# Where GpSimd puts its first sum: in its own room, or in the one that VectorE has just read

## The chip, the cores and the metric
The kernel runs on one core of one Trainium2 chip. The metric is the device time in microseconds. Three runs of the kernel before gave 2311.27, 2308.0 and 2311.83 us, median 2311.27 us. A further execution was taken with a profile, and its trace is what the views below show.

## The reference
An attention with 32 inducing points per batch is followed by a feed-forward layer with a rational activation:

```
s = scale * (I @ x^T);  h = softmax(s) @ x          # 4 batches, 12480 rows, 128 columns
y = softmax(scale * (x @ h^T)) @ h                   # 49920 rows in all
u = y @ w_in                                         # 128 -> 2048
g = (a0 + a1 u + a2 u^2 + a3 u^3) / (1 + |b0| |u| + |b1| u^2 + 1e-6)
out = g @ w_out                                      # 2048 -> 128
```

All of it is in float32, and the second part has most of the work.

## The kernel before
The 49920 rows are cut into 104 blocks of 480. A block's 2048 hidden columns are cut into eight units of 256, so there are 832 units, each a [128, 2, 480] tile. The loop `fast_ticks` takes one unit per tick `t`.

For unit `t`, TensorE writes u (folded with the attention, so that its input is the softmax weights) into one of three PSUM buffers named `hp`, one tick ahead. The absolute value goes into a slot of `row`: on VectorE where `t` is even (the `mask`, an integer AND), on ScalarE where it is odd. One tick later VectorE makes the unit's polynomial part, (row + k1) * hp, and puts it into a rung of `line`; that frees the `hp` buffer. `row` and `line` have twenty slots each and are used in a ring, so slot and rung of unit `i` are written again for unit `i+20`.

ScalarE then works on the slots of four units at a time: a logarithm and later a sigmoid, in place, three logarithms and three sigmoids for every twelve units, with two loads of the function table (`wide`).

In tick `i+17` (`BEHIND` is 17), for each four units `i` to `i+3`, `finals` makes line = (line + k3) * row. I call it the final of these units. VectorE makes that of the first two units in one instruction of 128x1920 elements, which reads two operands from SBUF. GpSimd makes that of the other two, unit by unit, with two instructions each: a sum (`tensor_scalar`, 128x960) and a product (`tensor_tensor`, 128x960). For the last four groups VectorE makes all of them. Two ticks after unit `i+2`'s own delay, in tick `i+21`, TensorE multiplies its rung with `w_out` into the buffer `po` (`second`); unit `i+3` follows in tick `i+22`.

The engines take their instructions in the order in which the program issues them; semaphores that the framework places from the overlap of the regions read and written are all that orders one engine against another. What is left over in a tick is given, in `side`, to work on the next batch: attention scores, exponentials, the quotient `a`/`asm` (on GpSimd: a small sum and a product), the stack `st` of the next weights (on GpSimd: a cast and a difference) and the transfers. The program fixes the order of all that when it is built, with costs written in the code.

The change is in `finals`. Before, the two GpSimd instructions of a unit both write the unit's rung `u.g`: the sum in place, and then the product of it with the slot `u.u`.

Of the kernel before, what the change touches and what calls it, by code (L numbers as in the profile page):

```python
# [17 lines left out]
ALU = mybir.AluOpType  # L18
# [187 lines left out]
class Kernel:  # L206
# [932 lines left out]
    def finals(self, units, i):  # L1139

        V, G, p = self.nc.vector, self.nc.gpsimd, self.params
        part = units[i:i + 4]
        own = 4 if i + BEHIND > len(units) else 2
        for k in range(0, min(own, len(part)), 2):
            a, b = part[k], part[min(k + 1, own - 1)]
            g, w = self.line[:, a.rung:b.rung + 1], self.row[:, a.slot:b.slot + 1]
            V.scalar_tensor_tensor(out=g, in0=g, scalar=p.z_k3, in1=w, op0=ALU.add, op1=ALU.mult)
        for u in part[own:]:
            G.tensor_scalar(out=u.g, in0=u.g, scalar1=1.0, scalar2=p.z_k3, op0=ALU.mult, op1=ALU.add)
            G.tensor_tensor(out=u.g, in0=u.g, in1=u.u, op=ALU.mult)  # L1150

    def general_ticks(self, units):
        V, A, G, p = self.nc.vector, self.nc.scalar, self.nc.gpsimd, self.params
# [172 lines left out]
```

## Time and profile before

| what | value |
|---|---|
| median of three runs | 2311.27 us (2308.0 to 2311.83) |
| the profiled execution's own time | 2307.58 us |
| its span, first to last instruction | 2305.7 us |
| granted TensorE clock, mean | 0.986 of full speed |
| VectorE busy | 2219.0 us, 96% |
| TensorE busy | 2130.3 us, 92% |
| ScalarE busy | 2061.2 us, 89% |
| GpSimd busy | 1786.6 us, 77% |

In the rows PE is TensorE, DVE is VectorE, ACT is ScalarE, POOL is GpSimd. A row of a timeline has the start in us from the start of the span, the duration in us, engine, line, operation, out<-in with the tiles' names, and in brackets the idle time of the engine before it and what ended that. A row of groups has the count, the busy time in us and the mean duration in ns. Nearly all instructions are issued through one helper, so all have its line, L190, and are told apart by tiles.

### The profile page before, as it was taken

Reading aid. Unit: us, or ns where it says so; the run is one execution under the profiler, and the core shown is the slowest. Engines: PE = TensorE matmul, PEld = TensorE weight load, DVE = VectorE, ACT = ScalarE, POOL = GpSimd, SP = SyncE. Lnnn points to the kernel's source line nnn. Section 1 sums busy time; section 2 is a strip of 40 time slices with the busy share of each in tenths; the row PEclk is TensorE's granted clock in tenths of the full one; section 3 lists DMA queues with packets and bytes.
Section 4 is the critical chain, followed back from the end, with each engine's and each line's share of the span. In section 5 each row is a group of like instructions: output and inputs, shape, how many; then the busy total and the mean of one; then the engine's idle time right before and its main releaser. Section 6 shows DMA issues by size and latency. Waiting matters only on the chain.

```text
span 2305.7 us, 22902 instructions
## 1 busy us (share of the span) xinstructions
PE 2130.3 (92%) x7728; PEld 967.6 (42%) x7728; DVE 2219.0 (96%) x2094; ACT 2061.2 (89%) x1085; POOL 1786.6 (77%) x1040
## 2 busy tenths in 40 slices
PE   5599999988999999998999999999999999999998
PEld 2244444434444444444444444444444444444444
DVE  7899999999999999999999999999999999999996
ACT  2589998988998999898998999999999999989996
POOL 1378687868887688788888768889887888878883
PEclk8799999999999999999999999999999999999999
DMA  8422031101223123100122203110110010000000
GB/s 313 129 69 68 24 89 48 35 29 41 69 73 90 35 55 84 36 22 30 35 88 88 73 22 86 48 40 18 55 48 17 22 52 19 25 18 22 18 18 19
DMA packets 105153, 125.03 MB, mean 54 GB/s; under 512 B 13378, under 2 KB 101314, under 8 KB 104514
## 3 DMA queue, kind: packets, MB, share of 16 engines
q1 hardware_dynamic: 105026, 123.48, 17.1%
q8 instruction: 63, 1.03, 0.2%
q14 instruction: 64, 0.52, 0.1%
HBM read 84.04 MB, written 26.61 MB: 48 GB/s over the span
## 4 chain that ended last, share of the span: by engine, by line
DVE 44%; PE 32%; issue 16%; ACT 4%; POOL 2%; DMA 1%; SPq 1%; DVEq 0%; POOLq 0%; ACTq 0%
DVE line L190 26%; PE po L190 21%; DVE row L190 11%; PE hp L190 8%; ACT row L190 3%; DVE oT L190 2%; POOL line L190 2%; PE ph L190 1%; DVE a L190 1%; PE pd L190 1%; PE pc L190 1%; DVE amx L190 1%; DVE hl L190 1%; DVE asm L190 1%; SPq L190 0%
## 5 line engine op out<-in xcount | busy, mean ns | idle before, releaser
L190 PE MATMUL po<-line,w_out 128*128 128x480 f32 x3328 | 1553.0, 572 | 3.9
L190 POOL TENSOR_TENSOR line<-line,row 128x960 f32<-128x960 f32 x408 | 1031.8, 2529 | 282.3 <-ACT row L190 229.3
L190 DVE SCALAR_TENSOR_TENSOR line<-row,all,hp 128x960 f32<-128x960 f32 x832 | 996.1, 1203 | 12.3 <-PE hp L190 11.0
L190 PEld LDWEIGHTS po<-line,w_out 128*128 128x128 f32 x3328 | 616.3, 190 | 404.5 <-issue 244.3
L190 ACT ACTIVATE row<-row,all 128x3840 f32<-128x3840 f32 x208 | 725.7, 3490 | 0.0
L190 ACT ACTIVATE row<-row 128x3840 f32<-128x3840 f32 x208 | 706.6, 3397 | 1.3 <-DVE line L190 1.3
L190 POOL TENSOR_SCALAR line<-line,all 128x960 f32<-128x960 f32 x408 | 668.5, 1639 | 3.6
L190 DVE SCALAR_TENSOR_TENSOR line<-line,all,row 128x1920 f32<-128x1920 f32 x212 | 608.6, 2873 | 19.9 <-ACT row L190 19.6
L190 PE MATMUL hp<-at,st 128*128 128x480 f16 x1664 | 477.0, 368 | 119.8 <-DVE line L190 112.2
L190 ACT ACTIVATE row<-hp,all 128x960 f32<-128x960 f32 x416 | 440.5, 1059 | 154.5 <-PE hp L190 150.0
L190 DVE TENSOR_SCALAR row<-hp 128x960 int32<-128x960 int32 x416 | 476.8, 1146 | 7.3 <-PE hp L190 7.0
L190 PEld LDWEIGHTS <-st 128*128 128x128 f16 x1872 | 181.8, 98 | 607.0 <-issue 594.9
L190 PE MATMUL hp<-same,by 96*128 96x480 f16 x832 | 240.6, 370 | 9.4 <-DVE row L190 8.5
L190 ACT ACT_TABLE_LOAD x140 | 179.6, 1283 | 3.2 <-PEq L1319 0.7
L190 PEld LDWEIGHTS <-by 96*128 96x128 f16 x832 | 82.4, 99 | 198.2 <-issue 177.9
L190 DVE TENSOR_SCALAR oT<-po,all 128x480 f32<-128x480 f32 x104 | 73.9, 710 | 20.1 <-PE po L190 20.0
L190 POOL TENSOR_SCALAR asm<-asm 120x16 f32<-120x16 f32 (+1 forms) x27 | 9.1, 336 | 68.0 <-DVE asm L190 65.1
L190 PE MATMUL po<-at,st 128*128 128x480 f16 x208 | 60.9, 375 | 0.0
L190 POOL TENSOR_TENSOR st<-gs,st 64x512 f16<-64x512 f32 x16 | 18.5, 1158 | 48.2 <-ACT st L190 47.1
L190 ACT ACTIVATE e<-e,nmc 128x960 f32<-128x960 f32 (+3 forms) x16 | 15.7, 979 | 28.5 <-DVE nmc L190 28.5
L190 POOL TENSOR_TENSOR a<-a,asm 120x512 f32<-120x512 f32 (+1 forms) x27 | 26.6, 985 | 2.9 <-DVE asm L190 2.9
L190 PE MATMUL pd<-xTb,HT 128*32 128x480 f32 x208 | 28.3, 578 | 0.4 <-issue 0.4
(117 smaller groups left out, 541.3 us busy)
## 6 DMA issues: line engine op xcount, KB each, us to landing
xTb<-x_c SPq DMA_DIRECT2D x104, 240.0 KB, 3.4
out<-oT SPq DMA_DIRECT2D x104, 240.0 KB, 2.0
xTa<-x_c SPq DMA_DIRECT2D x78, 240.0 KB, 3.0
x<-x_t SPq DMA_DIRECT2D x78, 240.0 KB, 4.2
at<-hl SPq DMA_DIRECT2D x416, 30.0 KB, 1.8
row<-x_c SPq DMA_DIRECT2D x8, 768.0 KB, 12.5
row<-x_r SPq DMA_DIRECT2D x8, 768.0 KB, 11.5
w_in<-kept SPq DMA_DIRECT2D x3, 1024.0 KB, 4.8
```

The lines of the kernel that those rows point to most:

```text
L190: ins = call(*args, **kw)
```

## The change
GpSimd's first sum of each group (that of unit `i+2`) is written into the row slot of unit `i`, which VectorE's final reads, and no longer in place. Its product reads the sum from there and writes `line` as before. The second unit's pair (`i+3`) is as it was. No instruction is added or removed. The first sum now has to follow VectorE's final, since it overwrites what that reads. The `mask` of unit `i+20`, which is the next writer of unit `i`'s slot, now has to follow GpSimd's first product, which reads it.

```diff
         for u in part[own:]:
-            G.tensor_scalar(out=u.g, in0=u.g, scalar1=1.0, scalar2=p.z_k3, op0=ALU.mult, op1=ALU.add)
-            G.tensor_tensor(out=u.g, in0=u.g, in1=u.u, op=ALU.mult)
+            t = part[0].u if u is part[own] else u.g
+            G.tensor_scalar(out=t, in0=u.g, scalar1=1.0, scalar2=p.z_k3, op0=ALU.mult, op1=ALU.add)
+            G.tensor_tensor(out=u.g, in0=t, in1=u.u, op=ALU.mult)
```

## Rows read from the trace of the kernel before

**Rows 1.** The page, busy time of each engine, share of the span, instructions.
```profile
PE 2130.3 (92%) x7728; PEld 967.6 (42%) x7728; DVE 2219.0 (96%) x2094; ACT 2061.2 (89%) x1085; POOL 1786.6 (77%) x1040
```

**Rows 2.** The tile `line`: count, shortest/median/longest ns, first and last start.
```profile
L190 POOL TENSOR_SCALAR line<-line,all x408: 1055/1070/3594, 99.8 to 2261.4; 128x960 f32<-128x960 f32 x136
L190 POOL TENSOR_TENSOR line<-line,row x408: 2212/2232/4378, 111.2 to 2264.4; 128x960 f32<-128x960 f32 x136
L190 DVE SCALAR_TENSOR_TENSOR line<-line,all,row x212: 2127/2572/4233, 111.1 to 2289.3; 128x1920 f32<-128x1920 f32 x106
```

**Rows 3.** Timeline of all engines, 2183 to 2207 us, chosen rows.
```profile
2183.67 2.21 DVE L190 SCALAR_TENSOR_TENSOR line<-line,all,row 128x1920 f32<-128x1920 f32 x1
2183.71 4.28 POOL L190 TENSOR_TENSOR line<-line,row 128x960 f32<-128x960 f32 x1 [3.00 <-ACT row L190]
...
2187.98 1.05 POOL L190 TENSOR_SCALAR line<-line,all 128x960 f32<-128x960 f32 x1
...
2189.12 2.23 POOL L190 TENSOR_TENSOR line<-line,row 128x960 f32<-128x960 f32 x1
...
2190.24 1.15 DVE L190 TENSOR_SCALAR row<-hp 128x960 int32<-128x960 int32 x1
...
2191.34 1.06 POOL L190 TENSOR_SCALAR line<-line,all 128x960 f32<-128x960 f32 x1
...
2192.43 2.22 DVE L190 SCALAR_TENSOR_TENSOR line<-line,all,row 128x1920 f32<-128x1920 f32 x1
...
2193.18 0.97 PE L190 MATMUL po<-line,w_out 128*128 128x480 f32 x2
...
2194.39 1.77 PE L190 MATMUL po<-line,w_out 128*128 128x480 f32 x4
...
2201.24 2.22 POOL L190 TENSOR_TENSOR line<-line,row 128x960 f32<-128x960 f32 x1
...
2201.81 3.67 DVE L190 SCALAR_TENSOR_TENSOR line<-line,all,row 128x1920 f32<-128x1920 f32 x1
...
2203.45 2.96 POOL L190 TENSOR_SCALAR line<-line,all 128x960 f32<-128x960 f32 x1
...
2206.66 0.56 PE L190 MATMUL hp<-at,st 128*128 128x480 f16 x2 [1.22 <-DVE line L190]
```

**Rows 4.** The page's costliest groups: VectorE's finals; busy us, mean ns.
```profile
L190 DVE SCALAR_TENSOR_TENSOR line<-line,all,row 128x1920 f32<-128x1920 f32 x212 | 608.6, 2873 | 19.9 <-ACT row L190 19.6
```

**Rows 5.** Waits of the whole span: total us, times, longest us.
```profile
POOL line L190 <- ACT row L190: 229.3, 61, 11.1
ACT row L190 <- PE hp L190: 150.0, 154, 2.8
```

**Rows 6.** VectorE's finals in 1014.15 to 1099.85 us, then in 1099.95 to 1180.80 us.
```profile
L190 DVE SCALAR_TENSOR_TENSOR line<-line,all,row 128x1920 f32<-128x1920 f32 x8 | 25.8, 3224 | 0.9 <-ACT row L190 0.9
...
L190 DVE SCALAR_TENSOR_TENSOR line<-line,all,row 128x1920 f32<-128x1920 f32 x8 | 18.0, 2250 | 0.6 <-ACT row L190 0.6
```

**Rows 7.** Busy us by stretch: its bounds, its length, then each engine (instructions).
```profile
1014.10:1099.90 85.80, 78.94 (x249) 35.59 (x248) 83.98 (x68) 78.39 (x39) 73.25 (x40) 0.98 0.11 35
1099.90:1180.82 80.92, 80.08 (x272) 36.81 (x271) 79.77 (x75) 77.58 (x40) 68.14 (x35) 1.00 0.18 57
2183.67:2212.18 28.51, 27.30 (x87) 12.80 (x86) 28.44 (x24) 28.45 (x15) 25.64 (x12) 1.00 0.06 18
200.00:2280.00 2080.00, 1965.63 (x6957) 893.89 (x6956) 2040.05 (x1746) 1933.82 (x994) 1690.80 (x958) 1.00 0.15 45
```

**Rows 8.** Timeline, 1232 to 1234 us: VectorE's sum `asm`, GpSimd released by it.
```profile
1232.40 0.67 DVE L190 TENSOR_REDUCE asm<-a 120x16 f32<-120x512 f32 x1
...
1233.17 0.20 POOL L190 TENSOR_SCALAR asm<-asm 120x16 f32<-120x16 f32 x1 [3.60 <-DVE asm L190]
```

**Rows 9.** GpSimd's largest side work, by shape: count, busy us, mean ns.
```profile
L190 POOL TENSOR_TENSOR a<-a,asm 120x512 f32<-120x512 f32 x23 | 24.1, 1049 | 2.9 <-DVE asm L190 2.9
L190 POOL TENSOR_TENSOR st<-gs,st 64x512 f16<-64x512 f32 x16 | 18.5, 1158 | 48.2 <-ACT st L190 47.1
```

## The prediction
> **What bounds the kernel now.** I read the page's busy shares first [rows 1]: VectorE is busy 96% of the span, TensorE 92%, ScalarE 89%, GpSimd 77%. The bound is VectorE, but "busy" hides waiting inside instructions, so next I took the tile `line` and compared the shortest with the longest duration of one form [rows 2]. VectorE's final, always 1920 elements, takes 2.13 to 4.23 us; GpSimd's sum 1.06 to 3.59, its product 2.21 to 4.38. The timeline shows why [rows 3]. At 2201.24 GpSimd starts a product that ends at 2203.46; VectorE's final, started at 2201.81, lasts 3.67, which is 2203.46 − 2201.81 + 2.02. GpSimd's next sum, started at 2203.45, lasts 2.96, about 1.9 more than an undisturbed one (1.05), and ends 1 us after the final. At 2183.67 it is the other way round: the final begins 0.04 before GpSimd's product and takes 2.21, and the product takes 4.28 instead of 2.23. So the final and a GpSimd instruction don't run side by side: whichever starts second stands until the other ends. VectorE's standing counts as busy, and it spreads: after the long final TensorE waits 1.22 us for VectorE's `line` (2206.66).
>
> Sum of it: the finals' mean is 2.873 us over 212 [rows 4]; undisturbed they take 2.21 [rows 3]. (2.873 − 2.21) × 212 = 140.6 us, 6.1% of the profiled execution's 2307.58.
>
> **What the change does, part by part.** The work is the same; only two waits are new. I follow one group from the start of VectorE's final.
>
> *The first sum waits for the final.* Today GpSimd runs by its inputs: the sum needs only `line`, so it starts ahead of the sigmoid, and GpSimd waits at the product (229.3 us in 61 waits [rows 5]), then drains the groups of a dozen units in a burst that falls across VectorE's finals at random. After the change each group starts at the final's end. A release from VectorE to GpSimd takes 0.10 us (1232.40 + 0.67 to 1233.17 [rows 8]). Then sum and product by their spacing in rows 3: 2187.98 to 2189.12 is 1.14, 2189.12 to 2191.34 is 2.22, again 1.14, and the last product 2.23. So GpSimd is done at 2.21 + 0.10 + 1.14 + 2.22 + 1.14 + 2.23 = 9.04 us. The next final comes at least 8.76 us after the last one in the best stretch (2183.67 to 2192.43), 9.38 in the group behind it (2192.43 to 2201.81), and 9.50 on the mean of its three groups (28.51 / 3 [rows 7]). The final thus meets an idle GpSimd nearly always; at 8.76 it stands 0.28.
>
> *Who is queued behind the waiting sum.* Behind it stand the rest of the group and the side work. The first product ends at 2.21 + 0.10 + 1.14 + 2.22 = 5.67, the second at 9.04. TensorE uses them at 2193.18 and within the burst of 2194.39 for the final of 2183.67 [rows 3], so at 9.5 and above 10.7: 3.8 and over 1.6 us of cover. Once that is gone TensorE waits, and three `hp` buffers later VectorE too.
>
> *The `mask` of unit i+20 waits for the first product.* In rows 3 the mask for the final of 2183.67 starts at 2190.24, 6.57 us later, without side work between. 6.57 − 5.67 leaves 0.9 us. The out-of-place sum, and a product that takes both operands from `row`, are in no row. Bounds for each sum: at best the in-place one's shortest, 1.06, at worst its longest, 3.59 [rows 2], which is one stood through a final. I take 1.07, the median, for the work per element is the same. At the other end the chain would be 2.5 longer and the mask would wait 1.6.
>
> *GpSimd's side work.* It now falls behind the group's products, from 9.04 on, just ahead of the next final. The two largest kinds are 1.05 and 1.16 us long, 23 and 16 of them [rows 9]. Bounds: nothing, or all of it, 24.1 + 18.5 = 42.6 us. Around 10 us of group time, a job of 1.05 started at 9.04 is nearly over when the final comes; I take 8 us.
>
> Here the Trainium skill speaks against the change: its page SBUF — State Buffer (SBUF: two separate sides) says that whichever of a VectorE instruction with two SBUF inputs and a GpSimd one starts first holds the shared ports for its whole length. By that the small GpSimd jobs hold a final back just as the products do, and the sum would be the 42.6 us end in place of 8; rows 3 agree for the products, and no row here shows it for the small jobs.
>
> *How much of the 140.6 becomes time.* VectorE is not alone near the limit. Two neighbouring stretches of eight groups show it: with finals of 3.224 mean [rows 6] the stretch takes 85.80 us [rows 7], with 2.250 it takes 80.92. That is 4.88 us for 8 × 0.974 = 7.8 of standing saved, a share of 0.63. The second had more other VectorE work, 79.77 − 18.0 = 61.8 against 83.98 − 25.8 = 58.2; corrected for these 3.6, the share is 1.09. From the other side comes ScalarE: it is busy 1933.82 of 2080 us, and in the best stretch 28.45 of 28.51 [rows 7], so its waits for `hp` (150.0 us [rows 5]) are all that can be won before it is the bound. If it gets to 98%, 2080 − 1933.82 / 0.98 = 107 us go. I take a share of 0.8: 112 us, less 8 for the side work: 104 us. The profiled execution would take 2307.58 − 104 = 2203.6. The median of the runs lies 3.7 above the profiled one, so 2207 us.
>
> TensorE's 1965.63 of 2080 busy would cap the gain at 114 us if the share were to be believed. Rows 3 say that it overstates: a burst of two records counts 0.97 and one of four 1.77, so 0.80 for two more and 0.17 of tail each time; so TensorE is no cap of its own here. The Trainium skill (Perfetto Trace Analysis, Identifying the Most-Contended Engine) holds the matmul busy share for a bad measure of what is left; by the share the gain would end at 114 us, by the rule it need not.
>
> **Rivals.**
> *Neighbours take it over.* ScalarE's table loads and long functions leave it no slack, TensorE follows, and VectorE now waits for them where it stood before. For it: ScalarE is full in the best stretch. Against: the eight undisturbed groups of rows 6 did run 10.12 us each against 10.73. At a share of 0.35: 49 us, 2262 us.
>
> *It does not keep them apart.* Side work and a group that starts late push the second product into the next final; the standing stays at 0.66 per final with another partner. For it: 9.04 is longer than the shortest interval, 8.76. Against: the mean interval is 10 and more, GpSimd has 23% to spare [rows 1], and one late group can't pass it on, as the next starts from its own final. No gain: 2311 us.
>
> *Slower: the mask.* If the first product ends later than the mask's turn, VectorE stands at the mask in each of 204 groups (408 sums, two each [rows 2]). It decides from 0.9 us of delay on, and costs more than it saves from 0.9 + 0.69 = 1.6 on (140.6 / 204 = 0.69). With an out-of-place sum at the dear end the wait is 1.6 per group, 204 × 1.6 = 326 less 140: about 2497 us; with half that delay, 1.25, the wait is 0.35, and 204 × 0.35 − 112 is still a gain of 41. I price the rival at a wait of 0.9: 2311 + 204 × 0.9 − 112 = 2383 us. Against: nothing in rows 2 sets an undisturbed sum apart from 1.07.
>
> **Chances and range.** The forecast (a share of 0.6 to 1.1) 0.66: 84 to 155 us go, and 0 to 42.6 of side work comes back, of which I take none at the good end and 16 at the bad one: 2311 − 155 + 0 is 2156, 2311 − 84 + 16 is 2243; its own range is 2156 to 2243. Neighbours 0.18, 2243 to 2300. Not apart 0.07. Slower 0.09. The range that holds 8 in 10 leaves out the dear end and the very best: 2155 to 2260. A measurement of this kernel tells 0.2%, some 4.6 us. Faster 0.84, same 0.07, slower 0.09.
>
> **What will show it.** Right: the finals' mean falls to 2.2 to 2.3; GpSimd's sums have one duration near 1.07 and its products near 2.23; GpSimd waits for VectorE's `line` in about 200 places, and its wait for ScalarE's `row` is gone; ScalarE's busy share is above 95%. Wrong: finals still near 2.8; idle time of VectorE in front of the mask with GpSimd as releaser; VectorE's waits for ScalarE's `row` or TensorE's `hp` grown by tens of us. The prediction fails if the time is not below 2260.

## The result, and the profile after

The changed kernel takes 2227.66 us (median of four runs, 2224.62 to 2228.36) against 2311.06 us (median of four): ratio 0.9639, 95% interval 0.9622 to 0.9656. That is 83.4 us less; the forecast was 104 less. In a later comparison the same two gave 0.9658 (0.9644 to 0.9673).

The tile `line` after the change, in the columns of [rows 2]:

```profile
L190 DVE SCALAR_TENSOR_TENSOR line<-line,all,row x212: 2112/2214/3153, 111.0 to 2208.8; 128x1920 f32<-128x1920 f32 x106
L190 POOL TENSOR_SCALAR row<-line,all x204: 1059/1066/1087, 113.3 to 2182.3; 128x960 f32<-128x960 f32 x102
L190 POOL TENSOR_TENSOR line<-row x204: 2215/2231/2250, 114.5 to 2183.4; 128x960 f32<-128x960 f32 x102
L190 POOL TENSOR_SCALAR line<-line,all x204: 1055/1067/1091, 116.7 to 2185.6; 128x960 f32<-128x960 f32 x102
L190 POOL TENSOR_TENSOR line<-line,row x204: 2214/2237/2255, 117.9 to 2186.8; 128x960 f32<-128x960 f32 x102
```

All 816 GpSimd instructions of the finals now have one duration. The longest sum was 3594 ns and is 1091; the longest product was 4378 and is 2255. VectorE's final has a median of 2214 ns, where it was 2572. The page after, its busy shares, as in [rows 1], and its costliest groups, as in [rows 4]:

```profile
PE 2117.1 (95%) x7728; PEld 968.4 (44%) x7728; DVE 2103.8 (95%) x2094; ACT 2055.4 (92%) x1085; POOL 1456.0 (65%) x1040
...
L190 POOL TENSOR_SCALAR row<-line,all 128x960 f32<-128x960 f32 x204 | 217.6, 1067 | 603.8 <-DVE line L190 526.0
...
L190 DVE SCALAR_TENSOR_TENSOR line<-line,all,row 128x1920 f32<-128x1920 f32 x212 | 478.8, 2260 | 27.6 <-ACT row L190 27.5
L190 DVE TENSOR_SCALAR row<-hp 128x960 int32<-128x960 int32 x416 | 477.9, 1149 | 10.5 <-PE hp L190 7.4
```

The finals fell from 608.6 to 478.8 us, by 129.8. VectorE's busy time fell by 115.2 (2219.0 to 2103.8), and the span by 80.3 (2305.7 to 2225.4): VectorE's idle time grew from 86.7 to 121.6, by 34.9. So of the 129.8 us 80.3 left the span, 34.9 became idle time, and 14.6 went into other instructions of VectorE that take longer now, `mag` (6.0) and the polynomial parts (3.2) among them. GpSimd waits for VectorE's `line` 526 us at the first sum; it has the time for that, being 65% busy. Two groups of the changed kernel, VectorE and then GpSimd in order of time, as in [rows 3]:

```profile
2104.43 2.22 DVE L190 SCALAR_TENSOR_TENSOR line<-line,all,row 128x1920 f32<-128x1920 f32 x1 [0.27 <-ACT row L190]
...
2111.00 1.15 DVE L190 TENSOR_SCALAR row<-hp 128x960 int32<-128x960 int32 x1
...
2113.19 2.33 DVE L190 SCALAR_TENSOR_TENSOR line<-line,all,row 128x1920 f32<-128x1920 f32 x1
```

```profile
2106.75 1.07 POOL L190 TENSOR_SCALAR row<-line,all 128x960 f32<-128x960 f32 x1 [2.93 <-DVE line L190]
2107.90 2.23 POOL L190 TENSOR_TENSOR line<-row 128x960 f32<-128x960 f32 x1
2110.11 1.07 POOL L190 TENSOR_SCALAR line<-line,all 128x960 f32<-128x960 f32 x1
2111.26 2.24 POOL L190 TENSOR_TENSOR line<-line,row 128x960 f32<-128x960 f32 x1
```

The first sum starts 0.10 after the final's end (2104.43 + 2.22 = 2106.65). The last product ends at 2113.50, 9.07 after the final's start; the next final came after 8.76 and takes 2.33, 0.12 more than alone. Just that small overlap is left in this short interval.

What is near its limit now is to be read in a stretch, as in the last of [rows 7]; TensorE, its weight loads, VectorE, ScalarE, GpSimd:

```profile
200.00:2200.00 2000.00, 1947.72 (x6942) 892.84 (x6940) 1924.66 (x1742) 1923.80 (x992) 1376.62 (x960) 1.00 0.16 47
```

ScalarE went from 93.0% to 96.2% of the stretch, TensorE from 94.5 to 97.4%, VectorE from 98.1 to 96.2%.

### The profile page after: what moved, and what is told of

It is laid out like the page before. It is cut to its first block, busy times and chain, and to the rows that moved or that the text cites. A ratio compares the mean times of both kernels' runs of the same rounds, so it can differ in the third digit from the quotient of the medians.

```text
span 2225.4 us, 22935 instructions
## 1 busy us (share of the span) xinstructions
PE 2117.1 (95%) x7728; PEld 968.4 (44%) x7728; DVE 2103.8 (95%) x2094; ACT 2055.4 (92%) x1085; POOL 1456.0 (65%) x1040
## 4 chain that ended last, share of the span: by engine, by line
PE 46%; DVE 25%; ACT 14%; issue 10%; POOL 3%; DMA 1%; SPq 1%; DVEq 0%; ACTq 0%; POOLq 0%
PE po L190 31%; DVE line L190 14%; ACT row L190 12%; PE hp L190 11%; DVE row L190 6%; POOL line L190 2%; DVE oT L190 1%; ACT L190 1%; PE ph L190 1%; PE pc L190 1%; PE pd L190 1%; DVE amx L190 1%; SPq L190 1%; ACT e L190 1%; POOL row L190 1%
## 5 line engine op out<-in xcount | busy, mean ns | idle before, releaser
L190 DVE SCALAR_TENSOR_TENSOR line<-row,all,hp 128x960 f32<-128x960 f32 x832 | 999.3, 1205 | 27.9 <-PE hp L190 22.7
L190 POOL TENSOR_SCALAR row<-line,all 128x960 f32<-128x960 f32 x204 | 217.6, 1067 | 603.8 <-DVE line L190 526.0
L190 DVE SCALAR_TENSOR_TENSOR line<-line,all,row 128x1920 f32<-128x1920 f32 x212 | 478.8, 2260 | 27.6 <-ACT row L190 27.5
L190 DVE TENSOR_SCALAR row<-hp 128x960 int32<-128x960 int32 x416 | 477.9, 1149 | 10.5 <-PE hp L190 7.4
L190 POOL TENSOR_TENSOR line<-line,row 128x960 f32<-128x960 f32 x204 | 456.4, 2237 | 17.0
L190 POOL TENSOR_TENSOR line<-row 128x960 f32<-128x960 f32 x204 | 455.0, 2230 | 17.0
L190 POOL TENSOR_SCALAR line<-line,all 128x960 f32<-128x960 f32 x204 | 217.9, 1068 | 0.0
L190 POOL TENSOR_TENSOR st<-gs,st 64x512 f16<-64x512 f32 x16 | 24.2, 1515 | 48.3 <-ACT st L190 47.2
L190 POOL TENSOR_TENSOR a<-a,asm 120x512 f32<-120x512 f32 (+1 forms) x27 | 44.2, 1638 | 0.0
```

The lines of the kernel that those rows point to most:

```text
L190: ins = call(*args, **kw)
```

## The experiments

Each kernel was compared with the kernel before, run beside it on the same chip.

**The wait alone.** On the kernel before:

```diff
+        if part[own:]:
+            G.memset(part[0].u[:, 0, 0:1], 0.0)
         for u in part[own:]:
```

> The wait without the place: both sums stay in place as before, and GpSimd first writes one column of unit i's slot (128x1), which has to follow VectorE's final; its in-order queue then holds the pair back until then. Theory apart (the gain comes from GpSimd's pair running between the finals): as the changed kernel, 2228 us, ratio 0.960 to 0.968, finals' mean 2.2 to 2.3. Rival place (the gain comes from where the sum is written): as before, 2311, ratio 0.998 or more, finals' mean near 2.87 and sums of up to 3 us. If the mask's wait for the first product costs something in the changed kernel, this one, in which the mask follows only the column, is some us faster.

2223.1 us, ratio 0.9615 (0.9595 to 0.9634). The finals and GpSimd's in-place pair:

```profile
L190 DVE SCALAR_TENSOR_TENSOR line<-line,all,row x212: 2114/2210/3966, 112.3 to 2207.1; 128x1920 f32<-128x1920 f32 x106
L190 POOL TENSOR_SCALAR line<-line,all x408: 1057/1069/1094, 114.7 to 2183.9; 128x960 f32<-128x960 f32 x136
L190 POOL TENSOR_TENSOR line<-line,row x408: 2212/2236/2257, 115.8 to 2185.1; 128x960 f32<-128x960 f32 x136
```

With the sums in their old place GpSimd's durations are those of the changed kernel, and the gain is there whole. The wait does it. This kernel may even be the faster one: its 0.9615 stands against 0.9639 with intervals that overlap, and against the 0.9658 (0.9644 to 0.9673) of the later comparison with intervals that don't. Whether those few us are the mask's wait, as the expectation has it, stays open: in the profiles the mask waits for GpSimd 0.8 us in the changed kernel and 0.5 here.

**The place alone.** On the changed kernel:

```diff
             g, w = self.line[:, a.rung:b.rung + 1], self.row[:, a.slot:b.slot + 1]
+            if own == 2:
+                w = self.row[:, part[2].slot:part[3].slot + 1]
```

> The place without the wait: the first sum is written into unit i's slot as in the changed kernel, but VectorE's final reads the slots of units i+2 and i+3 in place of its own (same size, wrong values), so that GpSimd need not follow it. Theory apart: the finals stand again, mean 2.6 to 3.0, and the time is 2280 to 2330. Rival place: 2228, finals near 2.26.

2291.35 us, ratio 0.9918 (0.9892 to 0.9945), with the finals standing again:

```profile
L190 DVE SCALAR_TENSOR_TENSOR line<-line,all,row x212: 2114/2512/4256, 110.7 to 2273.0; 128x1920 f32<-128x1920 f32 x106
L190 POOL TENSOR_SCALAR row<-line,all x204: 1055/1067/3142, 110.8 to 2243.3; 128x960 f32<-128x960 f32 x102
```

The rival fell: a sum in another room alone leaves three quarters of the gain behind. The 19 us that it has are not free of a wait either: the first sum writes where ScalarE's sigmoid writes, and now follows it (GpSimd waits 250.2 us for ScalarE's `row` there; before, the product did, 229.3 us). How much of the 19 comes from that later start was not tried.

**No pair.** On the kernel before, GpSimd's finals are left out:

```diff
-        for u in part[own:]:
+        for u in []:
```

> The kernel before without GpSimd's sums and products of the finals (these units' finals are left out, no wait in their place). Nothing of GpSimd's meets the finals but side work. Theory neighbours (of the 140 us of standing that could go, about 60 did not become time because TensorE and ScalarE are next): about as the changed kernel, 2215 to 2230. Rival still in the way (GpSimd's pair, its waits or the side work behind it cost the changed kernel the rest): 2165 to 2195.

2205.19 us, ratio 0.9539 (0.952 to 0.9558): 106 us less than before, outside of both expectations and between them.

```profile
PE 2107.7 (96%) x7728; PEld 967.6 (44%) x7728; DVE 2081.5 (94%) x2094; ACT 2053.2 (93%) x1085; POOL 118.7 (5%) x224
```

The finals' sum is 468.1 us (2210 ns each), so all of the 140.6 is gone from VectorE, and yet 35 us of it don't become time. VectorE is idle for 122.2 us here (2203.7 of span less 2081.5), as in the changed kernel (121.6). So the other 22 us that part the two are busy time of VectorE: 10.7 in the finals, and 11.0 in two small instructions that come four times each, `mag` (1898 ns there, 181 here) and a 32x1 one on `all` (1181 and 148). Both theories hold a share.

**Neighbours relieved.** On the changed kernel, ScalarE's sigmoid halved; a quarter of the products with `w_out` left out; both; and both on the kernel before:

```diff
-            A.activation(w, w, AF.Sigmoid, bias=p.lnc, scale=-2.0)
+            A.activation(w[:, 0:2], w[:, 0:2], AF.Sigmoid, bias=p.lnc, scale=-2.0)
```

```diff
-            nc.tensor.matmul(self.po[:, 0:BT], self.w_out[:, fc, :], u.g[:, k], start=(fc == 0), stop=(fc == self.NF - 1 and not self.fast))
+            W = BT // (1 + k)
+            nc.tensor.matmul(self.po[:, 0:W], self.w_out[:, fc, :], u.g[:, k, 0:W], start=(fc == 0), stop=(fc == self.NF - 1 and not self.fast))
```

> The changed kernel with ScalarE relieved: each sigmoid covers two of its four units (the other two are left out), some 1.6 us x 208 = 333 us of ScalarE less. Theory neighbours (TensorE and ScalarE took over part of the gain): 2190 to 2215, VectorE's and TensorE's waits for ScalarE's row fall. Rival in the way (what is missing is lost between VectorE and GpSimd): 2222 to 2230.

> The changed kernel with TensorE relieved: of the second half of each unit only 240 of 480 columns are multiplied with w_out (the rest of that product is left out), 0.2 us x 832 = 166 us of TensorE less. Theory neighbours: 2185 to 2215. Rival in the way: 2222 to 2230.

> The changed kernel with both reliefs (half the sigmoid and a quarter of the w_out products left out). Theory neighbours: VectorE alone bounds, its 2104 us busy plus some 50 us of start and end: 2145 to 2170. Rival in the way: above 2200.

> The kernel before with both reliefs (the same parts left out). Theory neighbours: VectorE, with its standing, bounds at 2219 us busy plus some 50: 2255 to 2280, so that the change is worth 100 to 130 us here against 83 in the whole kernel. Rival in the way: the difference between the two relieved kernels stays at 83 or less.

| kernel | us | ratio to before (interval) |
|---|---|---|
| changed, ScalarE relieved | 2202.96 | 0.9539 (0.9523 to 0.9555) |
| changed, TensorE relieved | 2198.98 | 0.9526 (0.9511 to 0.9542) |
| changed, both | 2159.2 | 0.9344 (0.9329 to 0.936) |
| before, both | 2255.2 | 0.9776 (0.9739 to 0.9813) |

VectorE's finals, first in the relieved kernel before and then in the relieved changed one, each from its groups:

```profile
L190 DVE SCALAR_TENSOR_TENSOR line<-line,all,row 128x1920 f32<-128x1920 f32 x212 | 591.0, 2789 | 0.4 <-ACT row L190 0.4
```

```profile
L190 DVE SCALAR_TENSOR_TENSOR line<-line,all,row 128x1920 f32<-128x1920 f32 x212 | 482.8, 2279 | 2.1 <-ACT row L190 2.0
```

Without its neighbours' load the change saves 108.2 us of finals and 96.0 us of time, a share of 0.89; in the whole kernel it saves 129.8 and 83.4, a share of 0.64. So most of what is missing is the neighbours' doing. VectorE's idle time says the same: with the change it grew by 34.9 us in the whole kernel, and by 5.2 in the relieved one (56.5 to 61.7). The intervals make the 96 some 87 to 105 us, a share of 0.80 to 0.97. The granted clock was 0.961 of full speed in the relieved kernel before and 0.977 in the relieved changed one; what that is worth in the 96 was not tried. One relief alone gives the changed kernel 25 or 29 us, both give 68: ScalarE and TensorE lie close together. The difference of 96 is just short of the 100 to 130 expected, since the finals stand a little less in the relieved kernel before (2789 ns against 2873).

**A longer chain.** The first sum made twice, in the changed kernel (the diff) and, in place, in that with the wait alone:

```diff
+            if u is part[own]:
+                G.tensor_scalar(out=t, in0=u.g, scalar1=1.0, scalar2=p.z_k3, op0=ALU.mult, op1=ALU.add)
             G.tensor_scalar(out=t, in0=u.g, scalar1=1.0, scalar2=p.z_k3, op0=ALU.mult, op1=ALU.add)
```

> The changed kernel with the first sum made twice (one more 128x960 sum of 1.14 us per group), so that the first product ends 6.8 us and the second 10.2 us after the final's start; the mask's turn comes at 6.6 us at the earliest and at 7.6 to 7.8 on the mean. Theory small margin (the mask's wait is free in the changed kernel, and begins to cost here): VectorE waits for GpSimd before the mask in some 40 to 80 groups, 10 to 25 us in all, and is 10 to 30 us slower than the same delay with the mask free. Rival no price: equal to it.

> The same delay with the mask free: the kernel with the wait alone (sums in place, GpSimd held by one column written into unit i's slot) and the first sum made twice (k3 is added twice in these units). GpSimd ends 10.3 us after the final's start, when on the mean the next final is due at 10.2: theory apart says that the second product stands in the way of about half of the finals again, by some tenths of a us each: mean 2.35 to 2.6, time 2230 to 2255.

2298.53 us, ratio 0.9954 (0.9937 to 0.997), and with the mask free 2304.01 us, 0.9968 (0.9954 to 0.9983). The groups of the first, with the mask held, and then of the second:

```profile
L190 DVE SCALAR_TENSOR_TENSOR line<-line,all,row 128x1920 f32<-128x1920 f32 x212 | 543.9, 2567 | 14.7 <-ACT row L190 14.1
L190 DVE TENSOR_SCALAR row<-hp 128x960 int32<-128x960 int32 x416 | 477.2, 1147 | 46.0 <-POOL line L190 30.6 <-PE hp L190 14.4
```

```profile
L190 DVE SCALAR_TENSOR_TENSOR line<-line,all,row 128x1920 f32<-128x1920 f32 x212 | 558.1, 2634 | 16.5 <-ACT row L190 16.3
L190 DVE TENSOR_SCALAR row<-hp 128x960 int32<-128x960 int32 x416 | 476.5, 1146 | 18.4 <-PE hp L190 12.8 <-POOL line L190 4.2 <-issue 0.2
```

The mask does wait where it is held, 30.6 us in all, but this kernel is not the slower one, and the 10 to 30 us that I expected as the price of the mask's wait are not there. Its finals stand less (2567 against 2634 ns); it may be that a final which the mask has already delayed has less to wait for. The surprise is the size of the whole. I expected 2230 to 2255 for the second; 1.14 us more per group took back nearly all of the gain. It is standing again: against the kernel with the wait alone the finals take 75.8 us more (482.3 to 558.1), and the time is 80.9 longer. A chain that ends at 10.2 to 10.3 stands against finals due, with the wait alone, every 10.1 on the mean, in intervals from under 9 to over 12 us: each short interval is stretched to the chain, and no long one gets shorter. That reading is worked out from the intervals; no run tests it apart.

**ScalarE one tick earlier.** On the kernel with the wait alone:

```diff
-FIRST = 9
+FIRST = 8
```

> The kernel with the wait alone, and ScalarE's logarithms and sigmoids one tick earlier (FIRST is 8), to take away the 28 us in which the finals wait for the sigmoid. Theory ScalarE late: 2205 to 2222, the finals' wait for ScalarE's row below 10 us. Rival other wait: the logarithm now follows VectorE's polynomial part of the same tick, ScalarE and TensorE wait for it, and the time is 2223 or more.

2303.5 us, ratio 0.9968 (0.9956 to 0.998). The second theory holds:

```profile
L190 DVE SCALAR_TENSOR_TENSOR line<-row,all,hp 128x960 f32<-128x960 f32 x832 | 998.6, 1207 | 160.4 <-ACT row L190 152.4 <-PE hp L190 7.0
...
L190 DVE SCALAR_TENSOR_TENSOR line<-line,all,row 128x1920 f32<-128x1920 f32 x212 | 474.1, 2238 | 0.0
```

The finals' wait of 28 us is gone, and VectorE's polynomial part waits 152 us for ScalarE instead.

**Joined.** On the kernel with the wait alone, one sum and one product for both units:

```diff
-        for u in part[own:]:
-            G.tensor_scalar(out=u.g, in0=u.g, scalar1=1.0, scalar2=p.z_k3, op0=ALU.mult, op1=ALU.add)
-            G.tensor_tensor(out=u.g, in0=u.g, in1=u.u, op=ALU.mult)
+        if part[own:]:
+            a, b = part[own], part[-1]
+            g, w = self.line[:, a.rung:b.rung + 1], self.row[:, a.slot:b.slot + 1]
+            G.tensor_scalar(out=g, in0=g, scalar1=1.0, scalar2=p.z_k3, op0=ALU.mult, op1=ALU.add)
+            G.tensor_tensor(out=g, in0=g, in1=w, op=ALU.mult)
```

> The kernel with the wait alone, and the two units' sums joined into one of 128x1920 and their products into one: GpSimd's chain after a final is two instructions instead of four, and ends about 0.2 us earlier (8.8 instead of 9.04 us after the final's start). Theory chain length (what GpSimd's chain reaches beyond the next final's turn is what is lost to the kernel without the pair): 2213 to 2222. Rival held products (TensorE needs the first unit at 9.5 us at the earliest and gets it at 8.8 instead of 5.7, and a colliding product is twice as long): 2226 or more.

> The changed kernel itself, beside the joined one: 2225 to 2230, ratio 0.962 to 0.966, all theories.

Joined: 2215.45 us, ratio 0.96 (0.9585 to 0.9614). The changed kernel beside it: 2228.93 us, 0.9658 (0.9644 to 0.9673). The intervals don't touch: this version beats the kernel before and the changed one. From the kernel with the wait alone, out of which it is made (0.9615, 0.9595 to 0.9634, in an earlier comparison), it is not told apart, so what the joining itself gives is not shown.

```profile
L190 DVE SCALAR_TENSOR_TENSOR line<-line,all,row x212: 2112/2214/3466, 112.7 to 2203.9; 128x1920 f32<-128x1920 f32 x106
L190 POOL TENSOR_SCALAR line<-line,all x204: 1862/1869/1884, 115.2 to 2177.3; 128x1920 f32<-128x1920 f32 x102
L190 POOL TENSOR_TENSOR line<-line,row x204: 4265/4289/4317, 117.1 to 2179.2; 128x1920 f32<-128x1920 f32 x102
```

A joined sum takes 1.87 us where two started 1.14 apart and took 1.07, and a joined product 4.29. The pair's 6.7 us become some 6.2, and the finals' mean is 2245 ns against 2260 in the changed kernel and 2277 with the wait alone. TensorE did not miss the earlier product.

## Why the prediction was right, point by point

*The bound was VectorE's standing.* Right, and shown: take the pair out, or order it behind the final, and the finals take 2210 to 2277 ns; put the sum elsewhere without that wait and they are at 2808.

*One group's course.* Right to 0.03 us in the group shown: 0.10 for the release, 9.07 against 9.04 to the chain's end.

*The waits behind the sum.* Right: TensorE waited for GpSimd's finals 5 us in all, and of the mask's 10.5 us of idle only 0.8 were for GpSimd. Waits of the changed kernel, in the columns of [rows 5]:

```profile
POOL row L190 <- DVE line L190: 526.0, 162, 13.8
...
DVE line L190 <- ACT row L190: 31.9, 36, 2.7
...
DVE line L190 <- PE hp L190: 22.7, 31, 1.5
...
PEld po L190 <- POOL row L190: 3.1, 12, 0.8
...
DVE row L190 <- POOL line L190: 0.8, 1, 0.8
```

An out-of-place sum takes 1067 ns, at the cheap end of its bounds. The slower rival's mechanism exists, as the longer chain shows, but even with the chain 1.14 longer its waits came to 30.6 us in 56 places.

*GpSimd's side work, 8 us.* Right in size. The finals' sum is 478.8, and 212 undisturbed ones would be 468.1 at the 2.210 of the kernel with no pair: 10.7 us are left. By the timeline some 7 of them are in 20 finals that began while a side job ran, and some 4 in 24 that began before GpSimd's last product was over. One example, VectorE first and then GpSimd:

```profile
1074.41 3.01 DVE L190 SCALAR_TENSOR_TENSOR line<-line,all,row 128x1920 f32<-128x1920 f32 x1
```

```profile
1074.24 1.16 POOL L190 TENSOR_TENSOR st<-gs,st 64x512 f16<-64x512 f32 x1
```

The final comes 0.17 after a small product of the stack and stands to its end at 1075.40. So a small GpSimd job holds a final back just as the large ones do, which no row before had shown. The Trainium skill's rule (SBUF — State Buffer, SBUF: two separate sides) agrees with this row. The dear end of 42.6 us did not come: 16 finals met a job of the two kinds in [rows 9], and stood 0.43 us each on the mean, since more than half of the job was over. The other way round, twelve jobs with these names stood behind a final and took 2.5 to 3.3 us.

*The share, 0.8.* This is the term that was mis-sized. It came out at 83.4 / 129.8 = 0.64, at the lower bound that the two stretches of [rows 6, 7] had given uncorrected. I had raised it because the better stretch had more side work, and taken ScalarE to 98%; it got to 96.2%, with TensorE at 97.4% beside it. The relieved kernels show that these two take most of the rest: 0.89 without their load. That TensorE is "no cap of its own" did not hold: with TensorE alone relieved the changed kernel is 29 us faster, with ScalarE alone 25. The 14.6 us of VectorE's other instructions were in no term. In the sum the whole miss is in the share: 129.8 × (0.8 − 0.64) = 20.8 us, against 104 − 83.4 = 20.6.

*The signs.* The finals' mean and GpSimd's durations came as forecast. GpSimd waits for VectorE's `line` in 162 places rather than about 200 (23 more are put down to TensorE's `hp`), and its wait for ScalarE's `row` fell from 229.3 to 5.6 us. *ScalarE above 95%* holds for the steady stretch, not for the page's 92%, which has the start and the end in it. One sign of being wrong came in part: VectorE's waits for `row` and `hp` grew by some 24 us, from 20.3 and 11.0 to 31.9 and 22.7 for `line`. They are part of the 34.9 us of idle time, and the mark of the neighbours. Before the change they were:

```profile
DVE line L190 <- ACT row L190: 20.3, 21, 2.7
...
DVE line L190 <- PE hp L190: 11.0, 20, 1.2
```

*The rival "not apart"* was given 0.07 and is nearer than I thought: 1.14 us more in GpSimd's chain, and the kernel is at 0.995 or above. "Neighbours" was right in its mechanism and wrong in its size (a share of 0.35). The range's lower end, 2155, is below the forecast's own best of 2156, so at that end it left out nothing.

## What to carry to other kernels

An engine that is busy 96% can be standing inside its instructions: compare the shortest and the longest duration of one form, and look at what runs on the other engine at the same time. A wait that keeps two engines' conflicting instructions apart can be a gain, if the waiting one's whole chain fits into the interval; here 1.14 us more per group took nearly all of it back. A saving on the bound engine is worth its full size only until the next engines are reached, and here they were 5 to 7% from full.

## What was not expected of the hardware

- GpSimd's two-operand product of 1920 elements takes 4.29 us against two of 2.23, and the sum 1.87 against two of 1.07: joining saves 0.17 and 0.27 us.
- VectorE's `mag`, 128x32 with both operands in SBUF, four times in the kernel, went from a mean of 407 ns to 1898: it too can stand behind a GpSimd instruction. Here GpSimd's product ends at 607.51, and `mag` at 607.56:

```profile
605.28 2.23 POOL L190 TENSOR_TENSOR line<-line,row 128x960 f32<-128x960 f32 x1
605.56 2.00 DVE L190 SCALAR_TENSOR_TENSOR mag<-HT 128x32 f32<-128x32 f32 x1
```
